# Attention and a gated feed-forward in one kernel: the first batch in three transfer sets, the others a batch at a time, groups up to 5 turned over on TensorE, stores one step later

## The chip, the cores and the metric

One core of one Trainium2 chip. The metric is the device time of one execution in microseconds (us), lower is better. A kernel was run once under the profiler, and several times for its time, in rounds that alternate with the kernel before on the same chip. Some executions of any kernel are slower by one to two per cent; only fast runs are compared.

## The reference, cut to what matters

```python
# q, k, v: (8 batches, 12 heads, 448 tokens, 64) float32
q_n, k_n = rmsnorm(q, g_q), rmsnorm(k, g_k)          # x / sqrt(mean(x*x) + 1e-6) * g
attn = softmax(q_n @ k_n^T / sqrt(64))               # (8, 12, 448, 448)
x = (attn @ v) with the heads put side by side       # (8, 448, 768)
h = relu(x @ w_in)                                   # w_in: 768 x 1024
u, v = h[..., :512], h[..., 512:]
v_s = w_spatial @ layernorm(v) + b_spatial           # mixes tokens, 448 x 448
out = (u * v_s) @ w_out                              # w_out: 512 x 768
```

## The kernel before: the parts that matter here

Four heads make a group, three groups a batch, 24 groups in all. A group's q and k are squared, summed, scaled and turned over (128x128 blocks transposed) before their scores can be computed. A group has seven passes of scores; two passes make a step, closed by one exponential of 128x1792 on ScalarE. Steps 0 to 9 are done pass by pass, with smaller exponentials; from step 10 on the loop below runs. TensorE, ScalarE, VectorE, GpSimd and SyncE each run their own instructions in the order in which the program emits them, so one that waits holds those behind it (below, ScalarE for 4.67 us).

Loading. Groups 1 to 6 come one at a time through a pool of three buffers, whole batches only later:

```python
qk_pool = early_sb.enter_context(tc.tile_pool(name="qk", bufs=3, side="right"))

def load(G, i, eng=sync):                  # one group of q (i=0) or k (i=1), 0.46 MB in 4 transfers
    b, g = divmod(G, NG)
    lo, hi = lo_hi((q_g, k_g)[i][b][g])
    t = qk_pool.tile([P, 2, NCH, D], FP, name="kf" if i else "qf")
    ...
def load_part(b, i, part):                 # a quarter of a whole batch of q or k
    ...
    sync.dma_start(out=(...)[part], in_=(...)[part])
def load_v(b, parts):                      # v of one batch, issued by GpSimd
    for i in parts:
        pool.dma_start(out=(...)[i], in_=(...)[i])

load_first(0, 0, sync); load_first(1, 0, act)
load_first(0, 1, sync); load_first(1, 1, act)
load(1, 0); load(2, 0); load(2, 1); load(3, 0); load(3, 1)
```

Turning over. On TensorE it costs seven transposes and a copy; as a transfer it costs a place in the queue of SyncE, and for the keys a scaling on VectorE afterwards (k_scale, from the tile kr):

```python
def transpose_pe(G, i, eng):
    ps = ps_w.tile([P, 8, 128], BF, name="ps")
    turn(ps, 0, nrm[G, i])                 # 7 matmuls with is_transpose
    (to_k if i else to_q)(t, ps, NCH, eng)
def transpose_dma(G, i):
    ...                                    # i == 1: t is a tile kr, scaled later
    sync.dma_start_transpose(out=..., in_=nrm[G, i]...)
```

The first steps, and the plan of groups 4 to 8 ("sq" squares, "red" sums, "sc" scaling, "tr" turning by transfer, "ks" scaling of the turned keys, "ldg" group load; numbers are steps):

```python
def early(p):
    if p == 0:
        squares(1, 1)
        load_v(0, range(4))
        load_w_in(1)
        ...
    elif p == 9:
        ...
        load_v(1, range(4))
    if p in (10, 11, 12):
        attend(0, (p - 11,))               # the attention of group 0: needs v of batch 0
...
FIRST = {4: {"red": (None, 10), "rstd": (11,), "sc": (11, 11), "tr": (11, 11), "ks": (13,)},
         5: {"sq": (10, 11), "red": (11, 12), "rstd": (13,), "sc": (13, 14), "tr": (14, 14), "ks": (16,)},
         6: {"sq": (13, 14), "red": (14, 15), "rstd": (16,), "sc": (16, 17), "tr": (17, 17), "ks": (20,)},
         7: {"ldg": (12, 12), "sq": (15, 17), "red": (17, 18), "rstd": (19,), "sc": (19, 19), "tr": (19, 20),
             "ks": (23,)},
         8: {"ldg": (15, 15), "sq": (18, 20)}}
...
for s in range(S0, NST):
    scores(pss[:, 0:2], 2 * s)
    scores(pss[:, 2:4], 2 * s + 1)
    prep(s, True)
    expo(pss, 2 * s, 2)
    prep(s, False)
    ...
```

Of the kernel before, what the change touches and what calls it, by code (L numbers as in the profile page):

```python
# [19 lines left out]
def kernel(  # L20
# [37 lines left out]
    first = early_sb.enter_context(tc.tile_pool(name="first", bufs=1, side="right"))  # L58
    qk_pool = early_sb.enter_context(tc.tile_pool(name="qk", bufs=3, side="right"))
    ps_e = early_pools.enter_context(tc.tile_pool(name="ps_e", bufs=2, space=PSUM, side="right"))  # L60
# [10 lines left out]
    m_pool = ctx.enter_context(tc.tile_pool(name="mp", bufs=1))  # L71
    o_pool = ctx.enter_context(tc.tile_pool(name="op", bufs=3))

# [9 lines left out]

    def load(G, i, eng=sync):
        b, g = divmod(G, NG)
        lo, hi = lo_hi((q_g, k_g)[i][b][g])
        t = qk_pool.tile([P, 2, NCH, D], FP, name="kf" if i else "qf")
        tv = t.rearrange("p h c d -> p h (c d)")
        raw[G, i] = t
        eng.dma_start(out=tv[0:64, :, 0:256], in_=lo[:, 0:2])  # L90
        eng.dma_start(out=tv[64:128, :, 0:192], in_=hi[:, 0:2])
        eng.dma_start(out=tv[64:128, :, 192:448], in_=lo[:, 2:4])
        eng.dma_start(out=tv[0:64, :, 256:448], in_=hi[:, 2:4])

# [43 lines left out]
    load_first(1, 1, act)  # L138
    load(1, 0)
    load(2, 0)  # L140
    load(2, 1)
    load(3, 0)
    load(3, 1)

# [254 lines left out]
    def recip(G):  # L399
        lr = r_pool.tile([P, S], FP, name="lr")  # L400
        rc = r_pool.tile([P, S], FP, name="rc")
        act.activation(out=lr, in_=pst.pop((G, -1))[:, 0:S], func=AF.Ln, bias=0.0, scale=1.0)  # L402
        act.activation(out=rc, in_=lr, func=AF.Exp, bias=0.0, scale=-1.0)  # L403
        rec[G] = rc
# [7 lines left out]

    def attend(G, parts=(-1, 0, 1)):
        for part in parts:
            weigh(G, part)
            if part < 0:
                recip(G)
        for part in parts:
            if part >= 0:
                xt_store(G, part)  # L420

# [94 lines left out]
    out_hi = [out[b][256:S].rearrange("(p c) m -> c p m", c=3) for b in range(B)]  # L516

    def unit_o(b, c, half, split=False):
        t0, m = tokens(c)
        o = P - m  # L520
        r = slice(384 * half, 384 * half + 384)

        def mms(ps, f):
            if half == 0 and f == 0:
                osb[b, c] = o_pool.tile([P, DM], FP, name="osb")
            pe.matmul(out=ps[o:o + m, 0:384], lhsT=gts[b][f][:, t0:t0 + m],  # L526
                      rhs=w_out[:, f, r], start=(f == 0), stop=(f == 3), tile_position=(0, o))

        def done(ps):
            t = osb[b, c]  # L530
            copy(t[o:P, r], ps[o:P, 0:384])
            for rr in ((r,) if split else (slice(0, DM),) if half else ()):
                if c < 3:
                    sync.dma_start(out=out_lo[b][c][:, rr], in_=t[0:64, rr])
                    sync.dma_start(out=out_hi[b][c][:, rr], in_=t[64:P, rr])
                else:
                    sync.dma_start(out=out_lo[b][c][:, rr], in_=t[64:P, rr])

        return unit(4, 0.163, mms, done)
# [45 lines left out]
    squares(0, 1, 0)  # L585
    load(1, 1, pool)
    reduce(0, 0, 0)
# [18 lines left out]
    def pass_scores(p):  # L606
        psp[p] = ps_e.tile([P, 2, 512], FP, name="pse")
        scores(psp[p], p)


    def early(p):
        if p == 0:
            squares(1, 1)
            load_v(0, range(4))
            load_w_in(1)
            squares(2, 1)
            load_w_in(0)
            transpose_first(0, 1, dve)
            transpose_first(1, 1, dve)
        elif p == 1:  # L620
            squares(1, 0, eng=act)
        elif p == 2:
            reduce(1, 0)
            reduce(1, 1)
        elif p == 3:
            rstd(1)
            scaled(1, 0, eng=dve)
            scaled(1, 1, eng=dve)
        elif p == 4:
            squares(2, 0, eng=act)  # L630
        elif p == 7:
            reduce(2, 0)
            reduce(2, 1)
        elif p == 9:
            rstd(2)
            scaled(2, 0, eng=dve)
            scaled(2, 1)
            squares(3, 0)
            squares(3, 1)
            load_v(1, range(4))  # L640
        elif p == 14:
            reduce(3, 0)
            reduce(3, 1)
        elif p == 15:
            rstd(3)
            scaled(3, 0, eng=dve)
            scaled(3, 1)
            squares(4, 0)
            squares(4, 1)
            load_w_sp()  # L650
        elif p == 19:
            reduce(4, 0)
        if p in (10, 11, 12):
            attend(0, (p - 11,))
        if p in (16, 17, 18):
            attend(1, (p - 17,))
        if p not in (0, 6, 10, 11, 12, 13, 16, 17, 18):
            dummies(6)

    pass_scores(0)  # L660
    for p in range(2 * S0):
        expo(psp[p], p, 1)
        if p in (6, 13):
            transpose_pe(p // NCH + 1, 0, dve)
            transpose_pe(p // NCH + 1, 1, dve)
        if p in (4, 5):
            load(4, p - 4)
        if p in (10, 11):
            load(5, p - 10)
        if p in (16, 17):  # L670
            load(6, p - 16)
        if p + 1 < 2 * S0:
            pass_scores(p + 1)
        early(p)
# [4 lines left out]
    ODD = {"sq": (-9, -7), "red": (-6, -5), "rstd": (-3,), "sc": (-3, -2), "tr": (-2, -1), "ks": (2,)}  # L679
    FIRST = {4: {"red": (None, 10), "rstd": (11,), "sc": (11, 11), "tr": (11, 11), "ks": (13,)},  # L680
             5: {"sq": (10, 11), "red": (11, 12), "rstd": (13,), "sc": (13, 14), "tr": (14, 14), "ks": (16,)},
             6: {"sq": (13, 14), "red": (14, 15), "rstd": (16,), "sc": (16, 17), "tr": (17, 17), "ks": (20,)},
             7: {"ldg": (12, 12), "sq": (15, 17), "red": (17, 18), "rstd": (19,), "sc": (19, 19), "tr": (19, 20),
                 "ks": (23,)},
             8: {"ldg": (15, 15), "sq": (18, 20)}}
    todo = {}
    for m in range(2, NGT // 2):
        for G, form in ((2 * m, EVEN), (2 * m + 1, ODD)):
            plan = {what: tuple(7 * m + o for o in os) for what, os in form.items()}
            if G in FIRST:  # L690
                plan = dict(plan if G == 8 else {}, **FIRST[G])
            for what, os in plan.items():
                for i, s in enumerate(os):
                    if s is not None:
                        todo.setdefault(s, []).append((what, G, i))
    SC8 = 23
    for b in range(3, B):
        first_q = max(15 if b == 3 else SC8 + 1, (21 * b - 38) // 2)
        for n in range(4):
            todo.setdefault(first_q + n // 2, []).append(("ld", NG * b, n))  # L700
            todo.setdefault(first_q + 2 + (n if b % 2 == 0 else n // 2), []).append(("ld", NG * b, n + 4))

    ORDER = ("red", "rstd", "sc", "sq", "tr", "ks", "ldg", "ld")

    def prep(s, early_act):
        for what, G, i in sorted(todo.get(s, ()), key=lambda x: (ORDER.index(x[0]), x[1:])):
            if (what == "rstd") != early_act:
                continue
            if what == "ld":
                load_part(G // NG, *divmod(i, 4))  # L710
            elif what == "ldg":
                load(G, i)
            elif what == "sq":
                squares(G, i)
            elif what == "red":
# [3 lines left out]
            elif what == "sc":  # L719
                scaled(G, i)  # L720
            elif what == "tr":
# [9 lines left out]
    for s, b in gate_step.items():  # L731
        if b + 2 < B:
            v_step.update({s + 4 + i: (b + 2, [i]) for i in range(4)})
    busy = {attend_step(G) for G in range(NGT)}
    early_pools.close()
    ps_sc = ctx.enter_context(tc.tile_pool(name="ps_sc", bufs=1, space=PSUM, side="right", reuse_waits="tile"))
    pss = ps_sc.tile([P, 4, 512], FP, name="pss")
    transpose_pe(3, 0, dve)
    transpose_pe(3, 1, dve)
    rate = 0.0  # L740
    for s in range(S0, NST):
        if s == SC8 + 1:
            early_sb.close()
            qb_pools.append(ctx.enter_context(
                tc.tile_pool(name="qb1", bufs=1, side="right", reuse_waits="tile")))
        scores(pss[:, 0:2], 2 * s)
        scores(pss[:, 2:4], 2 * s + 1)
        prep(s, True)
        expo(pss, 2 * s, 2)
        prep(s, False)  # L750
        if s in v_step:
            load_v(*v_step[s])
        if s == 18:
            load_w_out()
# [12 lines left out]


    attend(NGT - 1)
    quota[0] = 2  # L770
# [40 lines left out]
```

## Time and profile before

| | before |
|---|---|
| median of the runs | 316.17 us (315.12 to 317.46) |
| profiled execution | 316.8 us |
| step 10 begins | 44.38 us |
| step 21 | 85.99 us |
| step 22 | 90.70 us |
| step 50 | 181.99 us |
| to the end from there | 134.8 us |

A step begins where its 128x1792 exponential does in ScalarE's timeline; the prediction says how this serves as a ruler. Two kernels can then be compared stage by stage. The scores and the exponential of a step are the same in both; the preparation of later groups is in part placed differently. The page itself is shown in the prediction.

### The profile page before, as it was taken

The numbers are of one execution on the slowest core, as the hardware profiler recorded it, in microseconds if no ns is written. First come the engines' busy times: TensorE is split into PE (matmuls) and PEld (weight loads), VectorE is DVE, ScalarE is ACT, GpSimd is POOL, SyncE is SP. The second block draws the span as 40 slices with busy tenths as digits, with TensorE's granted clock in tenths as the row PEclk, the third lists the DMA queues.
The fourth block names the chain that finished last, engine by engine and source line by source line (L and its number), as shares of the span: only waits on it lengthen the run. The fifth ranks groups of instructions, "written<-read, shape, count | busy, mean of one in ns | idle before, by whom it ended". The sixth has DMA issues, their size and how long they took to land.

```text
span 316.8 us, 6478 instructions
## 1 busy us (share of the span) xinstructions
PE 276.5 (87%) x2527; PEld 128.3 (40%) x2537; DVE 197.4 (62%) x340; ACT 212.2 (67%) x277; POOL 203.6 (64%) x182
## 2 busy tenths in 40 slices
PE   7648759996398999779999999979999999999994
PEld 6334323343143444334433444434434443444552
DVE  3784665655448495492885587676756854754652
ACT  2667856895177887656777788767777786775321
POOL 3497885999529999269767899569767940400300
PEclk9787987997789999997999999999999999999998
DMA  5999995589995999999969999999835591132156
GB/s 138 216 198 232 232 222 124 128 186 162 204 205 90 225 167 281 203 192 167 181 148 194 173 210 203 190 201 181 168 55 93 73 215 42 27 99 53 25 151 174
DMA packets 83200, 50.90 MB, mean 161 GB/s; under 512 B 47009, under 2 KB 79426, under 8 KB 83170
## 3 DMA queue, kind: packets, MB, share of 16 engines
q1 hardware_dynamic: 67186, 41.34, 65.4%
q0 software_dynamic: 15408, 8.73, 22.2%
q10 hardware_dynamic: 576, 0.43, 0.6%
q8 instruction: 20, 0.33, 0.4%
q14 instruction: 10, 0.08, 0.1%
HBM read 38.55 MB, written 11.01 MB: 156 GB/s over the span
## 4 chain that ended last, share of the span: by engine, by line
PE 39%; POOL 15%; DMA 14%; DVE 12%; ACT 9%; SPq 5%; issue 5%; POOLq 0%; DVEq 0%; ACTq 0%
PE ps L526 10%; PE ps L467 7%; POOL sqt L249 6%; ACT et L373 6%; PE ps L507 6%; PE pss L366 6%; PE ps L395 6%; DMA kb<-in_k_dram 4%; POOL n L276 4%; PE ps L497 4%; DVE ms L257 4%; DMA qf<-in_q_dram 3%; POOL vn L489 3%; DMA kf<-in_k_dram 2%; DMA kr<-n 2%
## 5 line engine op out<-in xcount | busy, mean ns | idle before, releaser
L373 ACT ACTIVATE et<-pss 128x1792 bf16<-128x1792 f32 x74 | 122.9, 1660 | 52.2 <-PE pss L366 48.8
L257 DVE TENSOR_REDUCE ms<-sqt 128x14 f32<-128x896 f32 x46 | 49.3, 1075 | 17.9 <-POOL sqt L249 17.3
L410 DVE TENSOR_TENSOR xt<-ps,rc 128x448 bf16<-128x448 f32 x48 | 28.1, 619 | 51.6 <-ACT rc L403 41.0
L366 PE MATMUL pss<-qT,kT 64*128 64x448 bf16 x254 | 39.5, 368 | 18.1 <-DVE kT L346 11.8
L526 PE MATMUL ps<-w_out,gt 128*128 128x384 bf16 (+1 forms) x256 | 48.8, 332 | 1.2 <-ACT rs L266 0.5
L467 PE MATMUL ps<-w_in_v,xt 128*128 128x512 bf16 (+1 forms) x182 | 45.4, 381 | 0.4
L395 PE MATMUL ps<-et,vt 128*32 128x448 bf16 x768 | 44.1, 369 | 1.7 <-ACT lr L402 1.7
L276 POOL TENSOR_TENSOR n<-qb,rs 128x896 bf16<-128x896 f32 x15 | 25.4, 1693 | 25.4 <-ACT rs L266 25.3
L497 PE MATMUL ps<-xt,w_in_u 128*128 128x448 bf16 x192 | 40.3, 354 | 0.8 <-ACT vs L436 0.8
L526 PEld LDWEIGHTS <-gt 128*128 128x128 bf16 (+1 forms) x256 | 24.5, 102 | 20.8 <-issue 7.8
L366 PEld LDWEIGHTS <-kT 64*128 64x128 bf16 x276 | 10.8, 94 | 51.3 <-issue 31.1
L249 POOL TENSOR_TENSOR sqt<-kb 128x896 f32<-128x896 f32 x15 | 25.1, 1682 | 9.6 <-DMA kb<-in_k_dram 9.6
L444 DVE COPY osb<-ps 128x384 f32<-128x384 f32 (+1 forms) x45 | 24.0, 554 | 9.3 <-PE ps L526 8.5
L485 POOL TENSOR_SCALAR nm<-mv 128x4 f32<-128x4 f32 x8 | 1.8, 230 | 42.9 <-DVE mv L476 42.9
L395 PEld LDWEIGHTS <-vt 128*32 128x32 bf16 x768 | 21.3, 101 | 20.0 <-issue 6.4
L346 DVE TENSOR_SCALAR_CACHE_REDUCE kT<-kr,g_col 128x896 bf16<-128x896 bf16 x20 | 22.7, 1134 | 9.6 <-DMA kr<-n 9.5
L507 PE MATMUL ps<-w_spT,vn 128*128 128x448 bf16 (+1 forms) x128 | 28.1, 364 | 0.1
L497 PEld LDWEIGHTS <-w_in_u 128*128 128x128 bf16 x192 | 17.3, 98 | 21.2 <-issue 7.5
L489 POOL TENSOR_SCALAR vn<-vs,nm,rv 128x512 bf16<-128x512 bf16 (+1 forms) x32 | 24.0, 764 | 2.7 <-ACT rv L484 1.7
L467 PEld LDWEIGHTS <-xt 128*128 128x128 bf16 (+1 forms) x192 | 17.7, 100 | 19.5 <-issue 5.4
L276 POOL TENSOR_TENSOR n<-kb,rs 128x896 bf16<-128x896 f32 x15 | 25.4, 1693 | 0.1
L249 POOL TENSOR_TENSOR sqt<-qb 128x896 f32<-128x896 f32 x15 | 25.2, 1678 | 0.0
(92 smaller groups left out, 371.4 us busy)
## 6 DMA issues: line engine op xcount, KB each, us to landing
out_dram<-osb SPq DMA_DIRECT2D x55, 192.0 KB, 3.9
qb<-in_q_dram SPq DMA_DIRECT2D x10, 384.0 KB, 6.1
kb<-in_k_dram SPq DMA_DIRECT2D x10, 384.0 KB, 9.8
vt<-in_v_dram POOLq DMA_DIRECT2D x16, 192.0 KB, 6.5
qb<-in_q_dram SPq DMA_DIRECT2D x10, 288.0 KB, 6.9
kb<-in_k_dram SPq DMA_DIRECT2D x10, 288.0 KB, 10.5
vt<-in_v_dram POOLq DMA_DIRECT2D x16, 144.0 KB, 5.8
qf<-in_q_dram SPq DMA_DIRECT2D x16, 128.0 KB, 3.4
```

The source lines that it names most:

```text
L249: pool.tensor_tensor(out=t, in0=x, in1=x, op=ALU.mult)
L257: dve.tensor_reduce(out=sqs[gk][:, key[1], :], in_=sqt.pop(key).rearrange("p h c d -> p (h c) d"), axis=AX.X, op=ALU.add)
L276: (eng or pool).tensor_tensor(out=t.rearrange("p c h d -> p h c d"), in0=raw[key], in1=rst[gk][:, key[1], :].rearrange("p (h c) -> p h c", ...
L366: pe.matmul(out=ps[:, h, 0:S], lhsT=kT[r, c0:c0 + 128], rhs=qT[r, :], start=True, stop=True, tile_position=(64 * h, 0))
L373: act.activation(out=ets[s][:, 2 * a:2 * a + 2 * m, :], in_=ps[:, 0:2 * m, 0:S], func=AF.Exp, bias=0.0, scale=1.0)
L395: pe.matmul(out=ps[32 * l:32 * l + 32, 0:S], lhsT=w, rhs=et_of(G, 3 if r == 3 else r + 4 * y, h), start=(r == 0), stop=(r == 3), tile_posi ...
L410: dve.tensor_tensor(out=xts[b][:, 2 * g + half, :], in0=pst.pop((G, half))[:, 0:S], in1=rec[G], op=ALU.mult)
L467: pe.matmul(out=ps[0:m, :], lhsT=xts[b][:, j, t0:t0 + m], rhs=w_in_v[:, j, :], start=(j == 0), stop=(j == 5), tile_position=(0, 0))
L489: pool.tensor_scalar(out=vn_t[b % 2][0:m, c, :], in0=vs[b][c][0:m, :], scalar1=nms[b][0:m, c:c + 1], scalar2=rvs[b][0:m, c:c + 1], op0=ALU ...
L497: pe.matmul(out=ps[:, 0:S], lhsT=w_in_u[:, j, 128 * f:128 * f + 128], rhs=xts[b][:, j, :], start=(j == 0), stop=(j == 5))
L507: pe.matmul(out=ps[:, 0:S], lhsT=vn_t[b % 2][0:kp, c, 128 * f:128 * f + 128], rhs=w_spT[0:kp, c, :], start=(c == 0), stop=(c == NT - 1))
L526: pe.matmul(out=ps[o:o + m, 0:384], lhsT=gts[b][f][:, t0:t0 + m], rhs=w_out[:, f, r], start=(f == 0), stop=(f == 3), tile_position=(0, o))
```

## The change

Its intent: fewer and larger loads, no waiting for one of three group buffers, less work for GpSimd, no turning of early groups through the busy transfer engines, and no SyncE waiting for an output copy. The first batch's groups 1 and 2 come as one "pair" set each for k and q, batch 1 is queued at once, batch 2 at step 10, batch 3 from step 16. v of batch 0 is held until the keys of group 1 are scaled: a one-element copy on GpSimd that reads those keys stands ahead of it. Not shown in the cut: w_in moves from pass 0 to passes 8 and 16, the attention of groups 0 and 1 is spread over four passes, and the squares of k of groups 6 and 7 go to ScalarE, two scalings (q of groups 4 and 5) to VectorE.

```diff
-    load(1, 0)
-    load(2, 0)
-    load(2, 1)
-    load(3, 0)
-    load(3, 1)
+    load_pair(1)
+    load_pair(0)
+    for n in range(8):
+        load_part(1, *divmod(n, 4))
...
+    def after(key):
+        t = st_pool.tile([1, 1], BF, name="one")
+        pool.tensor_copy(out=t, in_=nrm[key][0:1, 0, 0, 0:1])
...
         if p == 0:
             squares(1, 1)
-            load_v(0, range(4))
-            load_w_in(1)
             squares(2, 1)
-            load_w_in(0)
...
             scaled(1, 0, eng=dve)
             scaled(1, 1, eng=dve)
+            after((1, 1))
+            load_v(0, range(4))
...
+    TURN = {5: (1, 0), 6: (1, 1), 11: (2, 0), 12: (2, 1), 18: (3, 0), 19: (3, 1)}
...
-    FIRST = {4: {... "tr": (11, 11), "ks": (13,)},
-             5: {... "tr": (14, 14), "ks": (16,)},
-             6: {"sq": (13, 14), ... "sc": (16, 17), "tr": (17, 17), "ks": (20,)},
-             7: {"ldg": (12, 12), "sq": (15, 17), ... "sc": (19, 19), "tr": (19, 20), "ks": (23,)},
-             8: {"ldg": (15, 15), "sq": (18, 20)}}
+    FIRST = {4: {... "turn": (12, 13)},
+             5: {... "turn": (15, 16)},
+             6: {"sq": (14, 14), ... "sc": (17, 18), "tr": (18, 18), "ks": (20,)},
+             7: {"sq": (16, 17), ... "sc": (19, 20), "tr": (20, 20), "ks": (23,)},
+             8: {"sq": (18, 20), "red": (19, 21)},
+             9: {"sq": (21, 23), "red": (22, 24)}}
...
-    for b in range(3, B):
-        first_q = max(15 if b == 3 else SC8 + 1, (21 * b - 38) // 2)
+    for b in range(2, B):
+        first_q = {2: S0, 3: 16}.get(b, (21 * b - 36) // 2)
...
+                stores.append(lambda rr=rr: store(b, c, rr))   # issued by flush(), one step later
...
+        if s == 11:
+            load_v(1, range(4))
+        if s == 13:
+            load_w_sp()
-        if s == 18:
+        if s == 21:
             load_w_out()
```

## The prediction

> **What bounds the kernel now.** I read the page first: busy shares, then the forty slices.
>
> ```profile
> span 316.8 us, 6478 instructions
> PE 276.5 (87%) x2527; PEld 128.3 (40%) x2537; DVE 197.4 (62%) x340; ACT 212.2 (67%) x277; POOL 203.6 (64%) x182
> ...
> PE   7648759996398999779999999979999999999994
> ...
> PEclk9787987997789999997999999999999999999998
> DMA  5999995589995999999969999999835591132156
> ```
>
> A slice is 7.92 us; count from 0. TensorE is nearly solid from slice 18 (143 us) on; the holes are before: slices 1 to 5 (8 to 48 us), 9 and 10 (71 to 87), 16 and 17 (127 to 143). The granted clock falls in or just after each. So I asked for the busy time of each engine by stage:
>
> ```profile
> core 0: us, PE busy (x) PEld busy (x) DVE busy (x) ACT busy (x) POOL busy (x), PEclk, DMA share, GB/s
> 13.00:44.00 31.00, 22.39 (x259) 12.13 (x258) 20.67 (x26) 21.88 (x32) 26.24 (x26) 0.87 1.20 224
> 44.00:70.00 26.00, 24.19 (x217) 9.69 (x222) 15.95 (x26) 21.17 (x29) 21.24 (x18) 0.87 0.69 149
> 70.00:86.00 16.00, 8.63 (x73) 3.69 (x69) 6.32 (x12) 5.70 (x8) 13.71 (x11) 0.79 1.39 182
> ...
> 180.00:270.00 90.00, 84.35 (x785) 37.31 (x785) 60.98 (x104) 68.51 (x85) 62.20 (x51) 1.00 0.87 148
> ```
>
> From 180 us on, TensorE is busy 84.35 of 90 us: it is the bound. From 13 to 44 us nothing but the transfers is full (share 1.20). From 44 to 70 they run at only 149 GB/s, and from 70 to 86 they are full again while TensorE idles: traffic that could have moved earlier was held back.
>
> The exponentials of 128x1792, 74 of them, mark the steps; numbering them 10 to 83, as the program does, gives a ruler. Step 10 starts at 44.4 us, 21 at 86.0, 22 at 90.7, 50 at 182.0, 71 at 248.0. From 50 to 71 a step takes 66.0 / 21 = 3.14 us; from 10 to 50 it takes 137.6 / 40 = 3.44. Most of the excess sits at step 21. The timelines of ScalarE, VectorE, the transfer queue of SyncE, and GpSimd there, in that order:
>
> ```profile
> 85.99 1.66 ACT L373 ACTIVATE et<-pss 128x1792 bf16<-128x1792 f32 x1 [7.36 <-PE pss L366]
> ...
> 83.80 1.15 DVE L346 TENSOR_SCALAR_CACHE_REDUCE kT<-kr,g_col 128x896 bf16<-128x896 bf16 x1 [6.81 <-DMA kr<-n]
> ...
> 66.99 2.61 SPq L105 DMA_DIRECT2D qb<-in_q_dram  x4
> 69.77 3.10 SPq L340 DMA_TRANSPOSE qT<-n  x1
> 72.99 3.48 SPq L340 DMA_TRANSPOSE kr<-n  x1
> 76.51 3.59 SPq L105 DMA_DIRECT2D kb<-in_k_dram  x4
> ...
> 93.32 1.68 POOL L249 TENSOR_TENSOR sqt<-kb 128x896 f32<-128x896 f32 x1 [9.57 <-DMA kb<-in_k_dram]
> ```
>
> The softmax waited 7.36 us for scores, the scores for group 6's scaled keys, these 6.81 us for a transfer that turns the keys (kr). That was issued at 73.0 and landed at 83.8, 10.8 us against a median of 5.5, behind four whole-batch q loads and beside w_out and v. Then GpSimd stood 9.57 us, in order, on a k load for group 8, with group 7's scaling queued behind it.
>
> **What the Trainium skill says.** "DMA: Bandwidth & Descriptors", section "Issuing engines are not separate DMA queues": transfers from all issuers share the same 16 engines and interleave. The trace agrees: that k load took 13.7 us where the median of its kind is 9.8. The same page, "Rules for kernel authors", advises few large transfers; here the group loads of 128 KB cost SyncE some 0.6 us of issue each. "TensorE: Matmul & The Clock Gate", part 1, says that an idle window of about 3.4 us halves the clock until it has been busy as long again. The trace agrees: after the hole at 80 to 84 us the granted clock is 0.50 from 84 to 88 and 1.00 from 92, and a scores matmul ranges from 346 to 578 ns. So a hole costs more than its length. Part 4 of that page: a transpose on TensorE ends in PSUM and needs a copy. The trace has seven in 0.55 us warm, 0.94 cold, and copies of 0.61 and 0.68 us.
>
> **The change, part by part.**
>
> 1. Loads. Sixty small q and k loads issued by SyncE become 24 large ones, and four issued by GpSimd go (about 2.6 us of it). No load waits for one of three group buffers any more; batch 1 is queued at once, batch 2 from step 10. That fills the slack of 44 to 70 us. With w_out at step 21 in place of 18, and v two steps later, the keys of group 6 are turned with fewer neighbours.
>
> 2. Groups 4 and 5 turned on TensorE: 4 x 7 = 28 more transposes, about 4 x 0.55 = 2.2 us. Two fewer sets of six dummies give back 2 x 0.5 = 1.0 us. Four fewer turning transfers.
>
> 3. Four GpSimd operations move: two squares (1.68 us) to ScalarE at about 0.95, two scalings (1.69) to VectorE at 1.09. GpSimd, 21.2 of 26 us busy from 44 to 70, loses 6.7 us there. The 1.79 us that ScalarE waits at 73.8 for the statistics of group 7, whose squares came late from GpSimd, should go.
>
> 4. Stores are issued one step later, when their copy is done. SyncE waited 33.8 + 31.9 + 9.1 us on output copies, but mostly where TensorE stayed fed. I count nothing.
>
> 5. v of batch 0 waits until the keys of group 1 are scaled, instead of starting at 16.7 us.
>
> *To step 10.* The first loads and both pair sets are 0.92 + 2.29 = 3.21 MB; 1.1 MB of it have moved by 8 us as now, the rest at the 190 to 220 GB/s that the trace has from 8 to 24 us, so k (the first 2.06 MB) lands near 12.5 us (14.9 before) and q near 17.8 (before 14.4). ScalarE, in order, then squares q of group 1 about 3 us later. The chain squares, reduction, rstd, two scalings, transposes, copy is some 7 us, so the first pass of group 1 starts near 25.4 us, where it started at 24.5. Batch 1 (2.75 MB) and v (0.69 MB) land by about 34 us, against group 3's sums at 34: near the need. Its keys then reach step 10 at about 43.5 us (44.4 before). Gain 1 us, give or take 2.
>
> *Steps 10 to 21.* 41.6 us now. At 3.14 us eleven steps would take 34.5. The lighter first batch and the extra transposes about cancel. I leave 2.5 us for v of batch 1, issued only in step 11 and needed in step 14, and for what remains of the wait for kr. So 37.0: gain 4.6 us.
>
> *Step 21 to 22.* 4.7 us with a cold clock becomes about 3.2: gain 1.5.
>
> *Steps 22 to 50.* 91.3 us for 28 steps. Excess over 3.14 is 3.4 us. Some of it is GpSimd's backlog: after the 9.57 us stop, kr for step 35 was issued late and VectorE waited 2.74 us for it at 129.3. I credit 3.3.
>
> *After step 50.* TensorE bound, same instructions: 0.
>
> Sum: 1.0 + 4.6 + 1.5 + 3.3 = 10.4 us, so about 305.8.
>
> **The rivals.**
>
> A. The late data only moves. For it: transfers are full in both stages, the bytes are the same, and v, w_in, batch 2 and batch 3 now compete from 23 to 75 us. If v of batch 0 lands after 33 us or v of batch 1 after step 14, TensorE blocks in order, and the clock drops as well. Against: 149 GB/s from 44 to 70 leaves 26 x (220 - 149) = about 1.8 MB to move earlier, and GpSimd no longer stops on a load. This would leave 311 to 316.
>
> B. TensorE is the bound anyway. It is busy 276.5 of 316.8; with 1.2 us more transposes the holes are all there is. In steps 22 to 50 the pace is already within 0.12 us a step of the steady one, so the credit there may not come. Against: part of the 276.5 is at half clock. Only the two holes gained: about 309.
>
> C. Everything lands: no wait at 21, warm clock from 50 us, SyncE free of copies so that late steps gain too. Steps 10 to 50 at 3.05 us would be 122 us, 15.6 less, and the last part 1 to 2 less: about 299. For it: the schedule is visibly tuned against these waits. Against: even the steady stage has 6% holes, from VectorE's order, which is unchanged.
>
> **Range and chances.** The middle is 306.0. C gives the low end, 299.5; A the high end, 313.5. A 2% gain needs 309.8, which takes a little over half of the sum; I give that 0.72. Within 2%, by A or half of B, 0.25. Slower by over 2% needs new stalls of 17 us: 0.03.
>
> **What would show it.** Right: no gap over 4 us between ScalarE's exponentials near step 21, GpSimd's wait for kb gone, over 170 GB/s in the stage after step 10, clock near 1.0 through step 22, step 10 between 42 and 45 us, and the time from step 50 to the end, 134.8 us, the same within 1.5 us. Wrong: TensorE waiting for v, or for w_in, in steps 10 to 16; kr still the last releaser at step 21; ScalarE standing over 3 us on the q of group 1; or a last part that changes by several us, which would mean that the stores counted.

## The result, and the profile after

The changed kernel took 325.67 us (median of 4 fast runs, 324.60 to 326.21), the kernel before in the same rounds 316.81 (315.12 to 318.69). Ratios here are the mean time of one kernel's fast runs over the mean of the other's fast runs of the same rounds, so not quite the ratio of the medians. This one is 1.0274, with a 95% interval of 1.0205 to 1.0342: slower by over 2%. The prediction of 306.0 us, with 299.5 to 313.5 around it, was wrong in size and in sign: it foresaw a gain of 10.

The page of the changed kernel, to be laid beside the rows in the prediction (a slice is now 8.07 us):

```profile
span 322.8 us, 6428 instructions
...
PE   8528286979891999997999999979999999999994
...
PEclk9978778999998799999999999999999999999999
DMA  5999995968799999999999999998944296132156
```

The hole at slices 9 and 10 of the kernel before, around step 21, is gone. There are deeper ones at slices 2 and 4 (16 to 24 and 32 to 40 us), and a new one at slice 12 (97 to 105 us). The same stages by the ruler, in the kernel before (start to step 10 left out; the columns of a row are the stretch, its length, busy time and instructions of TensorE, its weight loads, VectorE, ScalarE and GpSimd, granted clock, transfer share and rate in GB/s):

```profile
44.40:86.00 41.60, 32.49 (x284) 13.30 (x288) 21.87 (x38) 26.85 (x36) 34.56 (x27) 0.84 0.95 161
86.00:90.70 4.70, 4.70 (x55) 1.91 (x51) 2.22 (x5) 3.16 (x6) 0.00 (x0) 0.64 1.19 250
90.70:182.00 91.30, 83.85 (x765) 36.42 (x768) 61.20 (x106) 67.34 (x85) 70.25 (x58) 0.98 1.07 183
182.00:316.80 134.80, 124.42 (x1078) 57.30 (x1081) 84.21 (x148) 88.31 (x113) 66.66 (x59) 0.99 0.67 127
```

and in the kernel after:

```profile
52.70:89.10 36.40, 31.50 (x312) 14.39 (x316) 26.17 (x40) 28.75 (x38) 31.46 (x29) 0.95 0.76 120
89.10:92.50 3.40, 3.40 (x57) 1.59 (x50) 1.58 (x3) 3.06 (x5) 3.39 (x4) 1.00 1.15 207
92.50:187.90 95.40, 83.32 (x763) 36.70 (x766) 61.61 (x107) 67.32 (x85) 71.76 (x60) 0.96 1.17 188
187.90:322.80 134.90, 124.46 (x1078) 57.30 (x1081) 84.31 (x149) 88.39 (x113) 67.38 (x61) 1.00 0.69 127
```

From the exact starts of the exponentials:

| stage | before | after | change | predicted change |
|---|---|---|---|---|
| start to step 10 | 44.38 | 52.69 | +8.31 | -0.9 |
| 10 to 21 | 41.61 | 36.37 | -5.24 | -4.6 |
| 21 to 22 | 4.71 | 3.47 | -1.24 | -1.5 |
| 22 to 50 | 91.29 | 95.41 | +4.12 | -3.3 |
| 50 to the end | 134.8 | 134.9 | 0.1 | 0 |

The sum, +6.0 us, is the difference of the two profiled executions; the timed runs differ by 8.9 at the median. (The profiled execution of the kernel before is the slowest of its four, that of the changed kernel the fastest.) Three stages came near what was predicted. Two went the other way, and together they make +12.4 us.

*The first hole.* TensorE waits for v of batch 0 in the attention of group 0. In its timeline of the kernel after (start, length, engine and line, operation, and in brackets the idle time before it and what ended it):

```profile
35.64 0.37 PE L394 MATMUL ps<-et,vt 128*32 128x448 bf16 x2 [2.49 <-DMA vt<-in_v_dram]
39.67 1.68 PE L394 MATMUL ps<-et,vt 128*32 128x448 bf16 x14 [3.66 <-DMA vt<-in_v_dram]
```

In the kernel before the same products ran without a wait at 29.5 us:

```profile
29.47 0.94 PE L395 MATMUL ps<-et,vt 128*32 128x448 bf16 x16
```

The scores of the next pass stand behind these products on TensorE, so ScalarE stands too. Its timeline after:

```profile
20.48 0.95 ACT L246 ACTIVATE sqt<-pair 128x896 f32<-128x896 f32 x1 [6.00 <-DMA pair<-in_q_dram]
...
43.60 4.16 ACT L372 ACTIVATE et<-pse 128x896 bf16<-128x896 f32 x5 [9.87 <-PE ps L394]
...
105.02 1.66 ACT L372 ACTIVATE et<-pss 128x1792 bf16<-128x1792 f32 x1 [7.91 <-PE pss L365]
```

The last line is the second hole, taken up below; the first is a wait of 6.00 us for q of group 1, where the prediction allowed 3.

When was v issued? GpSimd's timeline after:

```profile
25.70 0.18 POOL L631 COPY one<-n 1x1 bf16<-1x1 bf16 x1 [8.29 <-DVE n L275]
25.83 2.74 POOL L130 DMA_DIRECT2D vt<-in_v_dram  x4
```

All four transfers were issued by 28.6 us, 4.6 us before the first products stood waiting for them (from 33.15) and 7 before they got them. Where the time went is in the shares of the two queues: q1 carries SyncE's loads, q0 GpSimd's. The first two lines below are from 28 to 32 us, the next two from 32 to 36, the last two from 36 to 40 (packets, MB, share of the 16 engines; several packets are in flight on an engine, so shares can pass 100%):

```profile
q1 hardware_dynamic: 879, 0.74, 105.7%
q0 software_dynamic: 121, 0.06, 11.7%
...
q0 software_dynamic: 1452, 0.62, 126.8%
q1 hardware_dynamic: 221, 0.22, 22.0%
...
q1 hardware_dynamic: 910, 0.80, 113.4%
q0 software_dynamic: 27, 0.01, 2.1%
```

Until 32 us next to nothing of v moved. From 32 to 36 nearly all of its 0.69 MB did. The last 0.01 MB came after that beside 0.80 MB of SyncE's. What those loads were is in SyncE's transfer queue:

```profile
10.70 5.37 SPq L105 DMA_DIRECT2D qb<-in_q_dram  x4
16.12 7.15 SPq L105 DMA_DIRECT2D kb<-in_k_dram  x4
31.43 2.60 SPq L105 DMA_DIRECT2D qb<-in_q_dram  x4
34.13 6.07 SPq L105 DMA_DIRECT2D kb<-in_k_dram  x4
...
84.53 2.62 SPq L105 DMA_DIRECT2D kb<-in_k_dram  x4
87.26 3.69 SPq L339 DMA_TRANSPOSE qT<-n  x1
91.05 3.56 SPq L339 DMA_TRANSPOSE kr<-n  x1
```

The first two lines are batch 1, issued before v. The next two are batch 2. The program puts batch 2 in step 10, and step 10 began at 52.7 us; SyncE issued it at 31.4. What held it was not the step. Batch 2 takes the memory of the pair sets, and SyncE stood from 23.3 to 31.4 for their reader on VectorE, the scaling of group 2, which ended at 31.39. From VectorE's timeline, and from the table of SyncE's waits (in all, times, longest; so 8.1 us here, and the 29.5 later):

```profile
30.30 1.09 DVE L275 TENSOR_TENSOR n<-pair,rs 128x896 bf16<-128x896 f32 x1 [0.70 <-ACT rs L265]
...
SPq L105 <- DVE n L275: 37.6, 2, 29.5
```

With its memory free, SyncE issued batch 2 at once, 21 us before step 10.

A check by bytes: the first loads and the pair sets are 3.21 MB, batch 1 is 2.75, together 5.96 MB ahead of v. Of these 1.1 had moved by 8 us, and the rest at 203 GB/s (the rate that this trace has from 10 to 32 us) takes 24 us. That gives 32 us; v's first packets came at 31, its bulk from 32. The agreement is not a rule: with v early (below) v began at 22.2 us, when some 4.0 of the 4.6 MB issued ahead of it had moved.

*The second hole.* Step 24 began 10.1 us after step 23. VectorE in the kernel after:

```profile
103.21 1.15 DVE L345 TENSOR_SCALAR_CACHE_REDUCE kT<-kr,g_col 128x896 bf16<-128x896 bf16 x1 [7.79 <-DMA kr<-n]
```

It is the stop that the kernel before had at step 21, on turned keys, now on group 7's in place of group 6's. The last three lines of SyncE's queue above show what stands ahead: four large loads of k of batch 3 (1.38 MB) at 84.5, and the two turnings behind them.

### The profile page after: what moved, and what is told of

It reads as the page before. It is cut to its first block, busy times and chain, and to the rows that moved or that the text cites. A ratio compares the mean times of both kernels' runs of the same rounds, so it can differ in the third digit from the quotient of the medians.

```text
span 322.8 us, 6428 instructions
## 1 busy us (share of the span) xinstructions
PE 274.9 (85%) x2543; PEld 129.7 (40%) x2553; DVE 199.0 (62%) x342; ACT 213.6 (66%) x279; POOL 195.7 (61%) x175
## 4 chain that ended last, share of the span: by engine, by line
PE 41%; ACT 9%; DVE 8%; POOL 6%; DMA 6%; issue 2%; POOLq 0%; DVEq 0%; ACTq 0%
PE ps L547 9%; PE ps L473 8%; PE ps L513 7%; PE ps L394 6%; PE pss L365 6%; ACT et L372 6%; DMA w_out<-in_moe_w_out_dram 4%; PE ps L503 4%; DVE ms L256 3%; POOL sqt L248 2%; POOL vn L495 2%; DMA qT<-n 2%; DVE xt L408 1%; DVE s L481 1%; DVE osb L450 1%
## 5 line engine op out<-in xcount | busy, mean ns | idle before, releaser
L408 DVE TENSOR_TENSOR xt<-ps,rc 128x448 bf16<-128x448 f32 x48 | 27.9, 619 | 43.8 <-ACT rc L401 43.1
L365 PE MATMUL pss<-qT,kT 64*128 64x448 bf16 x254 | 38.4, 360 | 17.4 <-DVE kT L345 9.1
L473 PE MATMUL ps<-w_in_v,xt 128*128 128x512 bf16 (+1 forms) x182 | 47.0, 390 | 0.4
L275 POOL TENSOR_TENSOR n<-qb,rs 128x896 bf16<-128x896 f32 x18 | 30.5, 1694 | 24.8 <-ACT rs L265 24.7
L275 POOL TENSOR_TENSOR n<-kb,rs 128x896 bf16<-128x896 f32 x21 | 36.9, 1756 | 10.7 <-issue 9.9
L248 POOL TENSOR_TENSOR sqt<-qb 128x896 f32<-128x896 f32 x21 | 36.1, 1719 | 0.0
L248 POOL TENSOR_TENSOR sqt<-kb 128x896 f32<-128x896 f32 x19 | 31.8, 1681 | 0.0
L513 PE MATMUL ps<-w_spT,vn 128*128 128x448 bf16 (+1 forms) x128 | 27.2, 353 | 0.1
L473 PEld LDWEIGHTS <-xt 128*128 128x128 bf16 (+1 forms) x192 | 18.2, 102 | 19.7 <-issue 5.5
L345 DVE TENSOR_SCALAR_CACHE_REDUCE kT<-kr,g_col 128x896 bf16<-128x896 bf16 x18 | 20.4, 1136 | 8.9 <-DMA kr<-n 8.9
```

Source lines behind the costliest of these rows:

```text
L248: pool.tensor_tensor(out=t, in0=x, in1=x, op=ALU.mult)
L275: (eng or pool).tensor_tensor(out=t.rearrange("p c h d -> p h c d"), in0=raw[key], in1=rst[gk][:, key[1], :].rearrange("p (h c) -> p h c", ...
L365: pe.matmul(out=ps[:, h, 0:S], lhsT=kT[r, c0:c0 + 128], rhs=qT[r, :], start=True, stop=True, tile_position=(64 * h, 0))
L408: dve.tensor_tensor(out=xts[b][:, 2 * g + half, :], in0=pst.pop((G, half))[:, 0:S], in1=rec[G], op=ALU.mult)
L473: pe.matmul(out=ps[0:m, :], lhsT=xts[b][:, j, t0:t0 + m], rhs=w_in_v[:, j, :], start=(j == 0), stop=(j == 5), tile_position=(0, 0))
L513: pe.matmul(out=ps[:, 0:S], lhsT=vn_t[b % 2][0:kp, c, 128 * f:128 * f + 128], rhs=w_spT[0:kp, c, :], start=(c == 0), stop=(c == NT - 1))
```

## The experiments

Theories at the start. *T1*: v of batch 0 is late because it is issued late, behind loads queued whole and early; issue it early and step 10 comes back. *T2*: the loads of batch 2 that ran ahead delay it. *T3*: w_out, moved to step 21, delays the turned keys of group 7. *T4*: the k of batch 3 does. All times are medians of fast runs, and "before" is that of the same rounds.

### Batch 2 held back

A one-element transfer on SyncE that reads the scaled keys of group 3 stands ahead of batch 2.

```diff
             if what == "ld":
+                if G == 2 * NG and i == 0:
+                    hold = st_pool.tile([1, 1], BF, name="hold")
+                    sync.dma_start(out=hold, in_=nrm[3, 1][0:1, 0, 0, 0:1])
                 load_part(G // NG, *divmod(i, 4))
```

> The changed kernel, but the loads of batch 2 wait on the queue until the keys of group 3 are scaled (a 2-byte transfer that reads them is put ahead). Theory A (v of batch 0 lands at 39.7 us because the loads of batch 2, which nothing holds back, start at 31.4 us and share the engines): TensorE's wait for v (6.1 us) shrinks to under 3 us, step 10 starts near 49 us instead of 52.7, the whole is about 3.5 us faster than the changed kernel. Rival B (v is late only because it is issued at 25.8 us behind the loads of batch 1): the wait for v stays near 6 us, step 10 stays within 1 us of 52.7.

Measured: 332.28 us against 318.22, ratio 1.0439 (1.0347 to 1.0531). Slower than the change itself, which neither theory had expected of the total. The profiled execution was disturbed (653.7 us), so the kernel was run again later:

> The same kernel as e1_hold_b2, for a profile in the undisturbed state. If the loads of batch 2 had taken engines from v, TensorE's wait for v would be under 3 us here and step 10 before 50; then the loss comes later, with batch 2 landing late, between steps 11 and 21. If v is served only once the loads of batch 1 are, which this kernel does not touch, step 10 stays near 52 us, v still lands near 36 to 40 us, and the loss of 6 us is added between steps 11 and 21.

Measured: one run of 330.91 us, of unknown state, with a span of 329.1 in its profile and a mean clock of 0.94. Step 10 began at 49.66, 3.0 us earlier than in the change. Its waits on TensorE for v:

```profile
35.44 0.37 PE L394 MATMUL ps<-et,vt 128*32 128x448 bf16 x2 [2.43 <-DMA vt<-in_v_dram]
36.92 1.68 PE L394 MATMUL ps<-et,vt 128*32 128x448 bf16 x14 [1.11 <-DMA vt<-in_v_dram]
```

The first part of v came at the same time as in the change (35.4 against 35.6), the last part 2.75 us earlier (36.92 against 39.67). By this one trace T2 holds in part: batch 2 accounts for the tail of the wait and some 3 us of step 10; the rest was there before batch 2 was issued. What the held loads then cost, from ScalarE's timeline:

```profile
70.21 0.95 ACT L246 ACTIVATE sqt<-kb 128x896 f32<-128x896 f32 x1 [4.67 <-DMA kb<-in_k_dram]
```

The change had given ScalarE the squares of k of group 6. With batch 2 late they wait 4.67 us, in order, ahead of the exponential of step 15; step 14 took 10.97 us. Loads that run ahead do harm early and good later, and holding them back is no cure.

### v of batch 0 early

```diff
         if p == 0:
             squares(1, 1)
+            load_v(0, range(4))
             squares(2, 1)
...
-            after((1, 1))
-            load_v(0, range(4))
```

> The changed kernel, but v of batch 0 is issued right after the squares of group 1's keys (near 16 us, as before the change) and does not wait for the scaled keys. If the hold on v is the cause of the 9.9 us hole: TensorE waits less than 1 us for v, the q of groups 1 and 2 land 1 to 2 us later than 20.4, step 10 starts near 45 us instead of 52.7, the whole is about 8 us faster than the changed kernel. If the transfers are simply full (rival: the hole only moves to another load): step 10 stays above 50 us.

v was issued at 15.6 us, in place of 25.8. Measured: 317.20 us against 318.22, ratio 1.0006 (0.9920 to 1.0093). The loss of 2.7% is gone. Step 10 began at 44.35, 8.34 us earlier than in the change, and TensorE's products of group 0 had no wait:

```profile
33.01 0.94 PE L394 MATMUL ps<-et,vt 128*32 128x448 bf16 x16
```

The stage from 10 to 21 took 36.35 us here, as in the change (36.37), so the gain of that stage is not just work put off from the first hole. The stop before step 24 is still there, on VectorE and then on ScalarE:

```profile
93.60 1.15 DVE L345 TENSOR_SCALAR_CACHE_REDUCE kT<-kr,g_col 128x896 bf16<-128x896 bf16 x1 [6.56 <-DMA kr<-n]
```

T1 holds for the first hole, and says nothing of the second.

This trace also shows how the two queues share. From 24 to 30 us v's queue moved 1159 packets and SyncE's 1160: turn by turn. What was slow is the start. Read in windows of 0.2 us, v's first packets came 5.2 to 7.0 us after its issue where whole-batch loads of SyncE were queued ahead of it (the change 5.2, this run 6.6, and three runs below 6.8 to 7.0), and 1.3 to 1.5 where none were (the kernel before 1.5, and four runs below). So the delay of v in the change has two parts: against the kernel before it was issued 9.1 us later, and its start took 3.7 us longer.

### The hold alone, in the kernel before

Is the late issue enough, without the whole batches ahead of it? In the kernel before, v and w_in were held in the same way.

```diff
-            load_v(0, range(4))
-            load_w_in(1)
             squares(2, 1)
-            load_w_in(0)
...
+            one = st_pool.tile([1, 1], BF, name="one")
+            pool.tensor_copy(out=one, in_=nrm[1, 1][0:1, 0, 0, 0:1])
+            load_v(0, range(4))
+            load_w_in(1)
+            load_w_in(0)
```

> The kernel before the change, with the hold alone: v of batch 0 (and w_in after it) waits for the scaled keys of group 1. If the hold by itself makes the hole: ScalarE waits over 5 us at the first attention, step 10 starts 6 to 9 us later than 44.4, the whole is 6 us or more slower than before. If it takes the hold and the whole batches queued ahead (here only three groups' loads fit in the buffers): a wait of 1 to 3 us, the whole 0 to 3 us slower.

Measured: 319.34 us against 316.71, ratio 1.0072 (1.0003 to 1.0142). The profiled execution was a slow one, so its times are only a hint: v issued at 21.9 us, TensorE waiting 1.22 us for it. By the timed runs the hold alone costs some 2 us (0.0072 x 316.7 = 2.3). The change paid over 8, so the late issue alone does not explain it; with whole batches queued ahead of v it does. (In this slow profile v's first packets came 1.3 us after its issue, in the change 5.2.)

### w_out moved: the wrong neighbour

The prediction had counted w_out among the neighbours that delay group 6's keys. Two kernels test it: the change with w_out back in step 13, and the kernel before with w_out in step 11, long ahead of the stop.

```diff
         if s == 13:                        # the change
             load_w_sp()
-        if s == 21:
             load_w_out()
```

```diff
-        if s == 18:                        # the kernel before
+        if s == 11:
             load_w_out()
```

> The changed kernel, but w_out is loaded in step 13 instead of 21. Theory: the 7.9 us stop before step 24 is the turned keys of group 7 sharing the engines with w_out (cast, 768 KB, 12.9 us in flight). Then the time from step 23 to 24 falls from 10.1 to under 4 us and the whole is 6 to 7 us faster. Rival: the keys are late because of the k loads of batch 3 and of v that are queued before them: the stop stays above 5 us.

> The kernel before the change, with w_out loaded in step 11 instead of 18. If the stop goes where w_out goes: the 9.0 us from step 20 to 21 fall to under 5 us and the whole is 4 to 6 us faster than before, that is 311 to 313 us. If the stop is made by the four q loads of batch 3 ahead of the turned keys: 20 to 21 stays above 7 us and the whole within 1.5 us of before.

Measured: 325.13 us against 318.22, ratio 1.0217 (1.0117 to 1.0316), with the change; 316.61, ratio 0.9967 (0.9892 to 1.0043), with the kernel before. Neither total moved beyond its interval. For the change the total is all there is, since its profiled execution was slow (363.2 us); the 6 to 7 us that T3 promised did not come. In the kernel before, with w_out out of the way, VectorE's wait ahead of step 21 was not shorter than the 6.81 us of the prediction:

```profile
84.35 1.15 DVE L346 TENSOR_SCALAR_CACHE_REDUCE kT<-kr,g_col 128x896 bf16<-128x896 bf16 x1 [7.99 <-DMA kr<-n]
```

From 20 to 21 it took 10.6 us, not less than 9.0. T3 falls. That w_out's place costs nothing is not shown by this: it returns below as a wait of TensorE.

### k of batch 3 earlier, and later

In the change, k of batch 3 was issued in steps 16 and 17 (not 18 and 19), ahead of the turning of group 6:

```diff
-            todo.setdefault(first_q + 2 + (...), []).append(("ld", NG * b, n + 4))
+            todo.setdefault(first_q + 2 * (b != 3) + (...), []).append(("ld", NG * b, n + 4))
```

> The changed kernel, but the four k loads of batch 3 are issued in steps 16 and 17, with its q loads and ahead of the turning of group 6, instead of between the turnings of groups 6 and 7. Theory (transfers are served nearly in order of issue: the turned keys of group 7 wait for the 1.4 MB of k that were issued 3 to 6 us before them): the time from step 23 to 24 falls from 10.1 to under 5 us, step 20 to 21 grows by up to 2 us, the whole is 4 to 6 us faster than the changed kernel, near 320. Rival (v of batch 2 and w_out are in the way): step 23 to 24 stays above 8 us and the whole within 1.5 us of the changed kernel.

Measured: 322.34 us against 317.32, ratio 1.0167 (1.0099 to 1.0235). From 23 to 24 it took 2.5 us in place of 10.1: T4 holds. But 20 to 21 took 6.6 in place of 2.7, and 21 to 22 took 5.4 in place of 3.5. VectorE and ScalarE there:

```profile
91.47 1.15 DVE L345 TENSOR_SCALAR_CACHE_REDUCE kT<-kr,g_col 128x896 bf16<-128x896 bf16 x1 [3.98 <-DMA kr<-n]
```

```profile
93.65 1.66 ACT L372 ACTIVATE et<-pss 128x1792 bf16<-128x1792 f32 x1 [4.90 <-PE pss L365]
```

The large load went ahead of group 6's turning, and group 6's keys were late instead. The rest of the stage gained: with the stop before step 24 gone, 22 to 50 took 86.3 us, against 91.3 in the kernel before. In the kernel before it was the four q loads of batch 3 that stood ahead of group 6's turning (the prediction's lines at 66.99, 69.77 and 72.99). There batch 3 was put three steps later, behind the turning of group 6 (with the squares of group 9 moved later to fit).

```diff
-        first_q = max(15 if b == 3 else SC8 + 1, (21 * b - 38) // 2)
+        first_q = max(18 if b == 3 else SC8 + 1, (21 * b - 38) // 2)
```

> The kernel before the change, with the loads of batch 3 three steps later, behind the turning of group 6 (and the squares of group 9 two steps later, as in the changed kernel). If transfers are served nearly in order of issue, the 9.0 us from step 20 to 21 fall to under 5 us; the turning of groups 7 and 8 then waits instead, so the whole gains 0 to 4 us. If v or the turning itself is slow: 20 to 21 stays above 7 us.

Measured: 315.89 us against 316.71, ratio 0.9983 (0.9927 to 1.0039). The stop at 20 to 21 shrank from 9.0 us to 4.25, and VectorE did not wait for turned keys at all. But ScalarE now stopped before step 24:

```profile
90.93 1.66 ACT L373 ACTIVATE et<-pss 128x1792 bf16<-128x1792 f32 x1 [5.34 <-PE pss L366]
```

From 23 to 24 it took 7.5 us, from 24 to 25 5.5. This stop is another one. GpSimd stood before the squares of q of batch 3, and VectorE, in order, behind it:

```profile
85.21 1.68 POOL L249 TENSOR_TENSOR sqt<-qb 128x896 f32<-128x896 f32 x1 [6.38 <-issue]
...
86.92 1.09 DVE L257 TENSOR_REDUCE ms<-sqt 128x14 f32<-128x896 f32 x1 [5.47 <-POOL sqt L249]
```

The profile names no releaser for GpSimd ("issue"). The last two of these q loads were issued from 76.15 us on and took up to 8.2 us, so the late load is the likely one; that is argued, not shown. In both kernels, then, a group's turned keys wait when large loads of batch 3 are queued ahead of its turning; with the loads behind the turning, work on batch 3 seems to wait instead. Moving the loads moves the stop, and the total changes little.

### The parts together

v early and k of batch 3 early, the two diffs above in one kernel:

> The changed kernel with v of batch 0 issued at once and the k loads of batch 3 early. If the two stops are separate the gains add: about 8 from v and 4 to 6 from k, near 312 to 314 us, faster than before. If the second stop is fed by the first, 317 as with v alone.

Measured: 313.09 us against 317.32, ratio 0.9865 (0.9794 to 0.9935): faster than both kernels, by 1.35% against before. Step 10 at 44.02; from 20 to 21 it still took 5.6 us.

Next, the q of group 1 for which ScalarE waited 6.00 us. The pair sets were cut into groups, k and q of group 1 first; two heads of group 0, which the pair sets load a second time, are left out (0.46 MB less).

```diff
     load_pair(1)                           # now only makes the tile
     load_pair(0)
+    for g in range(1, NG):
+        load_group(g, 1)                   # 4 smaller loads each
+        load_group(g, 0)
```

> The changed kernel, but the first batch's loads go group by group (k and q of group 1, then of group 2, 16 loads of two heads, no head twice). ScalarE's 6.0 us wait for q of group 1 at 14.5 us should fall under 1.5 us, and the first pass of group 1 start near 24 us instead of 28.1. But v of batch 0 still lands after the loads of batch 1, near 38 us, so step 10 moves by 2 us at most and the whole is 0 to 2 us faster than the changed kernel. If the large sets were the main loss, step 10 would move by 4 us or more.

Measured, in the change alone: 323.34 us against 317.32, ratio 1.0218 (1.0137 to 1.0298). ScalarE no longer waited for q:

```profile
14.47 0.95 ACT L256 ACTIVATE sqt<-pair 128x896 f32<-128x896 f32 x1
```

and TensorE reached the attention of group 0 earlier, only to wait longer for v:

```profile
32.90 0.56 PE L404 MATMUL ps<-et,vt 128*32 128x448 bf16 x2 [5.79 <-DMA vt<-in_v_dram]
37.24 1.68 PE L404 MATMUL ps<-et,vt 128*32 128x448 bf16 x14 [3.78 <-DMA vt<-in_v_dram]
```

Step 10 began at 49.88, 2.8 us earlier than in the change (the smaller sum of bytes has a part in that). Much of what the wait for q had cost was hidden behind v. (v was issued at 20.4 us here, and from 28 to 35 us it took turns with SyncE's loads, among them batch 2, which was freed earlier too, at 25.4.) All three diffs together (v early, k of batch 3 early, groups first):

> The changed kernel with all three: groups of the first batch one by one, v of batch 0 at once, k of batch 3 early. With v out of the way the 4 us of group 1 show: step 10 near 41 us, step 24 under 5 us after 23, the whole 306 to 311 us, 2% faster than before. If the transfers simply have no room: 313 or more.

Measured: 313.69 us, ratio 0.9887 (0.9806 to 0.9969), step 10 at 43.18. No better than without the groups first; the expectation of 306 to 311 was missed. With v issued some 4 us earlier still (at 8.0 us against 12.1), right after the first squares:

```diff
 squares(0, 0, 0, eng=act)
 squares(0, 1, 0)
+load_v(0, range(4))
 reduce(0, 0, 0)
...
         if p == 0:
             squares(1, 1)
-            load_v(0, range(4))
```

> f4 (313.7 us), but v of batch 0 is issued right after the first squares, near 8 us, among the loads of groups 1 and 2. If transfers are served in order of issue: ScalarE waits under 2 us for q of groups 1 and 2, TensorE under 0.5 us for v, step 10 comes before 42.5 us (f4 43.2), the whole is 0 to 3 us faster than f4. If the sum of the bytes is what binds: step 10 stays at 43 to 44.

Measured: 312.12 us against 317.48, ratio 0.9877 (0.9793 to 0.9960), step 10 at 43.14. The expected step 10 below 42.5 did not come: by then the order is good, and the sum of bytes appears to set the start. That was argued, not tried with fewer bytes.

The last part: take groups 6 and 7 off the transfer engines as well, turned on TensorE (in v early with k3 early, then in the order of need).

```diff
-             6: {... "sc": (17, 18), "tr": (18, 18), "ks": (20,)},
-             7: {... "sc": (19, 20), "tr": (20, 20), "ks": (23,)},
+             6: {... "sc": (17, 18), "turn": (18, 19)},
+             7: {... "sc": (19, 20), "turn": (21, 22)},
```

> The version with v of batch 0 at once and k of batch 3 early (313.1 us), with groups 6 and 7 also turned on TensorE. If what is left of the stops near steps 21 and 24 is the turning of keys behind loads: the time from step 20 to 21 falls from 5.6 to under 4 us, 28 more transposes cost about 2 us, the whole is 2 to 4 us faster, near 310, 2% under the kernel before. If TensorE, being the bound, only takes on work: 313 or more.

> h3 with groups 6 and 7 turned on TensorE as in g1. 1 to 3 us faster than h3, near 310, which would be 2% under the kernel before. Rival: TensorE's extra transposes eat it, 312 to 314.

Measured: 313.41 us against 316.71, ratio 0.9887 (0.9801 to 0.9973); and 311.37 against 317.48, ratio 0.9870 (0.9788 to 0.9952). In the first, 20 to 21 took 2.5 us. In the second, which has the lowest median of all, ScalarE passes steps 21 and 22 with hardly a wait:

```profile
80.66 1.67 ACT L382 ACTIVATE et<-pss 128x1792 bf16<-128x1792 f32 x1 [0.82 <-PE pss L375]
84.70 1.67 ACT L382 ACTIVATE et<-pss 128x1792 bf16<-128x1792 f32 x1 [0.87 <-PE pss L371]
```

The stop moved once more: from 24 to 25 this kernel took 5.8 us, 3.0 in the first of the two. TensorE stood for w_out, which the change loads in step 21:

```profile
93.90 0.35 PE L557 MATMUL ps<-w_out,gt 128*64 128x384 bf16 x1 [2.73 <-DMA w_out<-in_moe_w_out_dram]
```

An earlier w_out, which did nothing for the total while other stops stood, was not tried with these parts. The kernel beats the kernel before by 1.3%, less than the 2% hoped for. The intervals of the five versions that beat the kernel before (v and k of batch 3 early, all three parts, the order of need, and the last two) overlap: that each of them is faster than it is shown, their order is not.

### Stores at once

```diff
                 stores.append(lambda rr=rr: store(b, c, rr))
-            if b == B - 1 or split:
-                flush()
+            flush()
```

> The changed kernel with the stores issued at once again, not one step later. I expect no difference: within 1.5 us of the changed kernel, 324 to 327. If the later stores help: 2 us or more slower than the changed kernel. If they cost: 2 us or more faster.

Measured: 326.56 us against 316.71, ratio 1.0323 (1.0272 to 1.0373). The change itself has 1.0274 (1.0205 to 1.0342), so no difference can be told from none. No effect of the later stores is seen.

## Why the prediction was wrong, point by point

- *"To step 10 ... Gain 1 us, give or take 2."* This is the step that failed. Step 10 came 8.3 us later. The failing term is "Batch 1 (2.75 MB) and v (0.69 MB) land by about 34 us, against group 3's sums at 34: near the need". There are three errors in it. First, the need: group 3's sums are the need of batch 1; v's own need was 33 us, as only rival A said. Second, the sum: 5.55 MB were left at 8 us, which at the prediction's own 190 to 220 GB/s end at 33 to 37 us, not before v's need; at the 203 of the trace, v begins at 32 and ends after 35. With batch 2 held, it landed at 36.9. Third, "batch 2 from step 10": SyncE issued it at 31.4 us, when the pair sets' memory came free, and the tail of v then landed at 39.7. v early took back 8.3 us of step 10, batch 2 held took back 3.0 (one trace), and the hold alone, without the batches ahead, cost some 2 of the total.
- *The waits for v make 6.15 us, and step 10 lost 8.3.* TensorE's clock was 0.59 from 38 to 45 us in the trace, and the products after the wait took 1.68 us for fourteen against 0.94 for sixteen. This agrees with what the prediction quotes from the skill on idle windows; how much of the remaining 2 us it is was not measured by itself.
- *"ScalarE, in order, then squares q of group 1 about 3 us later."* The mechanism was right, the size was twice that: 6.00 us. By bytes the sets were through at some 18.2 us; q came at 20.4, when 3.7 MB and not 3.2 had moved, so part of batch 1 seems to have gone along with them. With groups first the wait went, and gave 2.8 us of step 10, since v waited behind it.
- *"Steps 10 to 21 ... 37.0."* Measured 36.4, and again with v early. Right in size; the reason given is in part not what happened. The slack was not filled: the stage moved 120 GB/s, less than the 161 before and not the "over 170" of the prediction's signs, since batch 2 had come before it. The gain is the stop of 9.0 us at step 21, now 2.7, and that stop came back at step 24. The versions of the change without the stop before step 24 took 37.6 to 40.7 here.
- *"Step 21 to 22 ... about 3.2."* Measured 3.5. Right: no cold clock there (1.00 against 0.64).
- *"Steps 22 to 50 ... I credit 3.3."* It lost 4.1. The credit came: GpSimd's stop on a k load went, and steps 34 and 38 took 3.2 us less. (They were shorter by 2.8 with w_out early in the kernel before as well, so that the change's loads did this is not shown.) But steps 23 and 24 took 8.0 us more, which the prediction did not count: a step of 10.1 us, as group 7's turned keys stood behind k of batch 3. The prediction had looked for kr at step 21 only, and of the neighbours of group 6's keys it moved w_out and v, where it was batch 3's loads, the q loads of which its own reading had named. Moving w_out did not shorten the stop; moving the k load took it from step 24 back to step 21 in the change; moving batch 3 ended VectorE's wait for kr at step 21 in the kernel before. v was not moved by itself. (The k load on which GpSimd stood 9.57 us was that of group 9, not 8: kb holds batch 3.)
- *"After step 50 ... 0."* 134.9 against 134.8. Right, and *stores: "I count nothing"* is right too.
- *Rival A* named the mechanism word for word ("If v of batch 0 lands after 33 us ... TensorE blocks in order, and the clock drops as well") and then put 311 to 316 on it, as if only the gains could be lost. The same wait can also be new. That, and 0.03 for slower, was the misjudgement of the range. "Slower by over 2% needs new stalls of 17 us" holds only if every gain lands. Here, by the ruler, nearly all did, and the two stalls, 8.3 to step 10 and 8.0 in steps 23 and 24, came close to 17. Of its signs of being wrong two came: TensorE waited for v (before step 10 already), and ScalarE stood over 3 us on the q of group 1.
- With v and the k load put right, groups first, and groups 6 and 7 turned on TensorE, the stages are 43.1, 37.6, 4.0, 89.5 and 135.1 us in the profiled execution, against the predicted 43.5, 37.0, 3.2, 88.0 and 134.8. So part of the predicted gains can be had with these parts in another order: by the timed runs 1.3%, some 4 of the 10.4 us. The change as written did not have that order.

What stays open: why a transfer on another queue starts 5.2 to 7.0 us after its issue behind whole batches; and what would bring step 10 below 43 us, fewer bytes or something else.

## What to carry to other kernels

An issuing queue has no steps of its own: the place of a load in the program says only what it stands behind. So ask of every load which wait holds it (here, only the memory that it reuses), and count the bytes already issued ahead of a small urgent transfer, on all queues, before you delay it. Large loads queued early must stand in the order of need of everything that shares the transfer engines, also of what another engine issues. And where engines run in order, removing a stop can move it to what is late next: another group behind the same load (group 6 for group 7 here), or another load (w_out). Look there as well before you credit the gain.

## What the Trainium skill lacked or had wrong

- "DMA: Bandwidth & Descriptors", section "Queues, rings and completion order", says that each transfer engine takes turns between the queue rows it has work for, packet by packet. With v early, the trace agrees once v moves: 1159 packets of v against 1160 of SyncE's from 24 to 30 us. It lacks the start: in the change v was issued from 25.8 us on, its first packets came at 31.0, and from 28 to 32 us it moved 121 against 879. Over five runs with whole batches queued ahead the start took 5.2 to 7.0 us, over five without 1.3 to 1.5. Why was not settled.
- The same page, "Rules for kernel authors", advises few large transfers, and to issue early. It lacks the price: 2.75 MB of batch 1, issued early, stood ahead of 0.69 MB of v that was needed no later. Issuing v at 15.6 us in place of 25.8, ahead of part of that batch, took 8.3 us off step 10; cutting the pair sets into groups (sixteen loads for eight, with 0.46 MB less) took 2.8 us off it.
- "TensorE: Matmul & The Clock Gate", Part 4, gives some 275 to 390 ns for one transpose. In this trace seven in a row take 0.56 us warm and 0.93 us cold, so they overlap; the page lacks the figure for a row of transposes, which is the one needed to weigh turning a group on TensorE.
